# An own list scheduler, smaller first token groups, batched folds and reshaped v reads in a fused attention and GLU block

## The chip, the cores and the metric

The kernel runs on one core of one Trainium2 chip. The metric is the device time of one execution in microseconds (us), inputs and outputs in device memory. Most executions of a kernel agree within about one per cent (the widest fast runs here are 270.24 to 273.89 us). Now and then one execution takes about 1.4 ms; such a run counts as slow and stays out of all comparisons.

PE is the matmul engine (TensorE), PEld its weight loads, DVE the VectorE, ACT the ScalarE, POOL the GpSimd; SPq is the sequencer of the sync engine, which issues the DMAs of this kernel in order.

## The reference, cut to what matters

Sizes: 2048 tokens, model width 512, 32 heads of 16, FFN width 1792, all bfloat16. `_layernorm` has no weights.

```python
mod = (silu(c) @ w_mod).reshape(1, 6, 1, -1)       # sa, ca, ga, sb, cb, gb: one row of 512 each
h = _layernorm(x) * (1 + ca) + sa
x = x + ga * A(h, wqkv, wo)          # attention: every token sees itself and the tokens
                                     # 2, 4, ..., 14 before it (8 keys), softmax over these
h = _layernorm(x) * (1 + cb) + sb
x = x + gb * B(h, w_gate, w_up, w_down)            # (gelu(h @ w_gate) * (h @ w_up)) @ w_down
```

## The kernel before: the parts that the argument touches

Tokens are worked in four groups of 512. q, k and v stand transposed (features on partitions). A key shifted by 2 tokens is a column offset, so the logits of one attention are products of q with shifted k on VectorE, and then sums over the features of a head, made by PE with a 0/1 matrix of 32 columns. Four such narrow matmuls stand side by side in the array. I call four of them a *fold*.

```python
for j in range(4):                                   # attention, logits
    for wg in range(2):
        pq = prodpool.tile([P, 4, SG], BF16, name="pq", tag="prod")
        nc.vector.tensor_tensor(out=pq[:], in0=<q, broadcast>, in1=<k at 4 shifts>, op=ALU.mult)
        for r in range(4):                           # one fold
            nc.tensor.matmul(LT[wg][32 * r:32 * r + 32, :], lhsT=M[:], rhs=pq[:, r, :],
                             start=(j == 0), stop=(j == 3), tile_position=(0, 32 * r))
```

For the weighted sum of v, the heads have to stand on other partitions and v at four shifts. So v goes to DRAM and is read back, four transfers of 128 partitions for a group:

```python
nc.sync.dma_start(out=scr[:], in_=vT[:])
for j in range(4):
    src = bass.AP(scr.tensor, scr.offset + 2 + j * row, [[2, 4], [16 * row, H], [4 * row, 4], [1, VW]])
    nc.sync.dma_start(out=vRj[:], in_=src)           # 4 shifts x 32 heads x 4 features x 520 tokens
```

The scale `gb` is multiplied into the down projection once, on VectorE, within the first group's FFN:

```python
if sg == 0:
    nc.vector.tensor_tensor(out=WdP[:, ft, :], in0=WdP[:, ft, :], in1=gbB[:], op=ALU.mult)
```

The sequence of the groups, which the language's own scheduler then refines:

```python
for sg in range(NSG):
    emit_attention(sg)
    if sg == 0:
        emit_qkv(1); emit_ln1(2); emit_qkv(2); emit_ln1(3)
    elif sg == 1:
        emit_qkv(3)
    if sg >= 1:
        emit_ffn(sg - 1)
emit_ffn(NSG - 1, last=True)
```

## Time and profile before

| | before |
|---|---|
| median of the fast runs | 303.7 us |
| span of the profiled run | 302.1 us |
| PE busy | 264.5 us |
| first matmul of the FFN | 83.1 us |
| end of the last matmul | 298.4 us |

These lines are from the page of the kernel before: PE's busy time and instruction count, then busy tenths in 40 slices of 7.6 us, and the granted PE clock in tenths.

```profile
PE 264.5 (88%) x1476; PEld 113.3 (38%) x1476; DVE 172.9 (57%) x305; ACT 142.0 (47%) x238; POOL 18.1 (6%) x41
PE   7696986128399999998999899899989989999995
PEclk9699899555669999999999999999999999999999
```

From slice 12 on (counted from 1) PE is nearly full. The hole is in slices 7 to 11, and the clock is low in slices 8 to 12: what PE does there it does at 5 or 6 tenths of full speed. The windows view puts numbers to it. Its columns are busy us and instructions of PE, weight loads, DVE, ACT and POOL, then granted clock, DMA share and GB/s.

```profile
40.00:50.00 10.00, 8.64 (x54) 4.03 (x53) 5.06 (x6) 6.98 (x12) 0.23 (x1) 1.00 0.27 89
50.00:60.00 10.00, 2.03 (x16) 0.44 (x15) 4.76 (x4) 1.39 (x3) 1.04 (x1) 0.68 0.51 141
60.00:70.00 10.00, 3.08 (x13) 0.75 (x14) 4.63 (x4) 0.78 (x2) 0.00 (x0) 0.50 1.05 331
70.00:80.00 10.00, 6.72 (x29) 1.89 (x27) 8.26 (x16) 0.00 (x0) 0.70 (x1) 0.67 0.22 70
```

Neither PE nor DVE is full between 50 and 70 us, so both wait. The chain of work that ended last (start, duration, what) names the reason:

```profile
25.36 9.28 DMA scr<-vT
...
37.72 6.75 SPq L258
44.51 20.31 DMA vR<-scr
64.94 1.24 DVE pv L318
```

v of the first group is ready at 25.4 us, and its last piece is back at 64.8. Meanwhile the DMA moves only 89 GB/s (40 to 50 us).

Last, how a fold sits among other matmuls in PE's timeline (start, duration, operation, count):

```profile
159.18 1.04 PE L346 MATMUL g_ps<-h2T,Wg 128*128 128x512 bf16 x4
160.18 0.40 PE L276 MATMUL LT_1543<-pq,Mph 128*32 128x512 bf16 x4
160.51 1.04 PE L350 MATMUL u_ps<-h2T,Wu 128*128 128x512 bf16 x4
```

Read such lines by their starts, for matmuls overlap. Four gate matmuls after one another advance 0.866 us elsewhere in this timeline; here the fold starts 1.00 us after them, and the next group 0.33 us after the fold. A fold in a row of folds advances 0.2165 us. A lone one costs 0.33 + 0.13 = 0.46.

### The profile page before, as it was taken

The page shows a single profiled execution, that of the slowest core. Times are in us where ns is not written, and L with a number is a line of the kernel's source. Part 1 is how long each engine was busy: PE and PEld are TensorE (multiplying, and loading weights), DVE is VectorE, ACT ScalarE, POOL GpSimd, SP SyncE. Part 2 cuts the span into 40 slices and gives each one's busy share as a digit, 9 for nine tenths or more (in the row PEclk, how much of TensorE's full clock was granted, in tenths as well). Part 3 has the DMA queues.
Part 4 walks back from the last instruction along what each step waited for, and adds up shares of the span by engine and source line. Part 5 has one row for each costly group of instructions (what it writes and reads, how often), then busy time and mean ns, then how long its engine had stood idle before and what let it go on. Part 6 is the DMA issues. An engine that isn't in the chain of part 4 may idle for free.

```text
span 302.1 us, 3849 instructions
## 1 busy us (share of the span) xinstructions
PE 264.5 (88%) x1476; PEld 113.3 (38%) x1476; DVE 172.9 (57%) x305; ACT 142.0 (47%) x238; POOL 18.1 (6%) x41
## 2 busy tenths in 40 slices
PE   7696986128399999998999899899989989999995
PEld 3353342002144544344443333344333444444442
DVE  4481747347998328996228599843859852122221
ACT  1366364100168797646305864440685462166700
POOL 6120001000111000002000000200000010000000
PEclk9699899555669999999999999999999999999999
DMA  7999422694222122231220012100000000100000
GB/s 209 383 284 277 150 85 92 165 318 169 59 90 86 67 82 86 96 143 45 76 64 35 0 30 78 36 20 35 17 2 1 0 2 17 53 0 3 0 35 35
DMA packets 21032, 25.87 MB, mean 86 GB/s; under 512 B 661, under 2 KB 19350, under 8 KB 21014
## 3 DMA queue, kind: packets, MB, share of 16 engines
q1 hardware_dynamic: 21012, 25.63, 27.4%
q8 instruction: 11, 0.18, 0.3%
q14 instruction: 7, 0.06, 0.1%
q10 hardware_dynamic: 2, 0.00, 0.0%
HBM read 21.37 MB, written 4.26 MB: 85 GB/s over the span
## 4 chain that ended last, share of the span: by engine, by line
PE 65%; DMA 12%; DVE 11%; SPq 4%; ACT 3%; POOL 2%; issue 1%; POOLq 0%; DVEq 0%; ACTq 0%
PE u_ps L350 13%; PE y_ps L368 12%; PE qkv_ps L246 10%; PE g_ps L346 9%; DMA vR<-scr 7%; PE y_psb L368 4%; PE g_psq L346 4%; PE x_ps L329 4%; SPq L258 3%; PE o_ps L321 3%; DMA scr<-vT 3%; DVE st L183 3%; PE hTp L200 3%; DVE x_sg L331 2%; DMA wm<-in_w_mod_dram 2%; POOL rstd L187 2%
## 5 line engine op out<-in xcount | busy, mean ns | idle before, releaser
L350 PE MATMUL u_ps<-h2T,Wu 128*128 128x512 bf16 x224 | 62.6, 383 | 0.0
L246 PE MATMUL qkv_ps<-hT,wqkv 128*128 128x512 bf16 x192 | 49.3, 397 | 1.7 <-DVE hT L204 1.3
L346 PE MATMUL g_ps<-h2T,Wg 128*128 128x512 bf16 x168 | 49.3, 387 | 0.9 <-ACT h2T L207 0.9
L353 ACT ACTIVATE gl<-g_ps 128x512 bf16<-128x512 f32 x42 | 25.4, 604 | 42.6 <-PE g_ps L346 40.0
L318 DVE TENSOR_TENSOR pv<-e,vR 128x2048 bf16<-128x2048 bf16 x32 | 37.0, 1219 | 11.7 <-DMA vR<-scr 11.6
L273 DVE TENSOR_TENSOR pq<-qT,kT 128x2048 bf16<-128x2048 bf16 x32 | 37.9, 1212 | 6.4 <-PE LT_471 L276 6.4
L355 ACT CAST ub<-u_ps 128x512 bf16<-128x512 f32 x56 | 33.1, 591 | 18.0 <-PE u_ps L350 18.0
L357 DVE TENSOR_TENSOR hht<-gl,ub 128x512 bf16<-128x512 bf16 x56 | 23.0, 419 | 30.7 <-ACT ub L355 30.2
L368 PE MATMUL y_ps<-WdP,hht 128*128 128x512 bf16 x168 | 36.9, 379 | 0.0
L368 PEld LDWEIGHTS <-hht 128*128 128x128 bf16 x224 | 21.9, 98 | 26.2
L346 PEld LDWEIGHTS <-Wg 128*128 128x128 bf16 x224 | 21.0, 99 | 25.8 <-issue 5.3
L350 PEld LDWEIGHTS <-Wu 128*128 128x128 bf16 x224 | 20.7, 98 | 25.5 <-issue 5.1
L246 PEld LDWEIGHTS <-wqkv 128*128 128x128 bf16 x192 | 20.8, 117 | 23.8 <-issue 8.2
L321 PE MATMUL o_ps<-pv,F_157 128*32 128x512 bf16 x128 | 13.7, 416 | 14.5 <-DVE pv L318 14.4
L371 DVE TENSOR_TENSOR ot<-y_ps,x_sg 128x512 bf16<-128x512 f32 x12 | 8.3, 691 | 26.2 <-PE y_ps L368 21.6
L183 DVE BATCH_NORM_STATS2 st<-x_sg 128x6 f32<-128x512 bf16 x32 | 20.9, 672 | 3.8 <-DMA x_sg<-in_A_x_dram 3.8
L187 POOL TENSOR_TENSOR rstd<-rstd,neghalf 128x4 f32<-128x4 f32 x8 | 10.6, 1330 | 187.6 <-DVE rstd L186 187.6
L323 ACT CAST oT<-o_ps 128x512 bf16<-128x512 f32 x16 | 9.4, 586 | 23.2 <-PE o_ps L321 23.2
L329 PE MATMUL x_ps<-woP,oT 128*128 128x512 bf16 x64 | 18.8, 434 | 0.7 <-ACT oT L323 0.7
L207 ACT ACTIVATE h2T<-hTp,modT,scl 128x512 bf16<-128x512 bf16 x16 | 11.6, 787 | 14.7 <-PE hTp L200 14.6
L353 ACT ACTIVATE gl<-g_psq 128x512 bf16<-128x512 f32 x14 | 8.4, 597 | 14.6 <-PE g_psq L346 14.6
L346 PE MATMUL g_psq<-h2T,Wg 128*128 128x512 bf16 x56 | 14.4, 379 | 0.0
(134 smaller groups left out, 214.1 us busy)
## 6 DMA issues: line engine op xcount, KB each, us to landing
vR<-scr SPq DMA_DIRECT2D x16, 520.0 KB
wm<-in_w_mod_dram SPq DMA_DIRECT2D x6, 512.0 KB
scr<-vT SPq DMA_DIRECT2D x4, 528.0 KB
out_dram<-ot SPq DMA_DIRECT2D x16, 128.0 KB
Wg<-in_B_w_gate_dram SPq DMA_DIRECT2D x1, 1792.0 KB
Wu<-in_B_w_up_dram SPq DMA_DIRECT2D x1, 1792.0 KB
WdP<-in_B_w_down_dram SPq DMA_DIRECT2D x1, 1792.0 KB
wqkv<-in_A_wqkv_dram SPq DMA_DIRECT2D x3, 512.0 KB
```

Of the source, the lines that this page charges most:

```text
L183: nc.vector.bn_stats(out=st[:, c4, :], in_=xt[:, c4, :])
L246: nc.tensor.matmul(ps[:], lhsT=wqkv[:, dt, blk * D + j:(blk + 1) * D:4], rhs=hT[:, dt, :], start=(dt == 0), stop=(dt == DT - 1))
L273: nc.vector.tensor_tensor(out=pq[:], in0=_ap(qT[:, j, :], [[0, 4], [1, SG]]), in1=_ap(kT[:, j, :], [[2, 4], [1, SG]], offset=HALO - 6 - 8 ...
L318: nc.vector.tensor_tensor(out=pv[:], in0=_ap(e[:, wg, :], [[0, 4], [1, SG]]), in1=vR[j][:, :, 8 - 8 * wg:8 - 8 * wg + SG], op=ALU.mult)
L321: nc.tensor.matmul(o_ps[32 * d4:32 * d4 + 32, :], lhsT=F1[:], rhs=pv[:, d4, :], start=(wg == 0), stop=(wg == 1), tile_position=(0, 32 * d4))
L329: nc.tensor.matmul(x1_ps[:], lhsT=oT[:, j, c4 * P:(c4 + 1) * P], rhs=woP[:, j, :], start=(j == 0), stop=(j == 3))
L346: nc.tensor.matmul(g_ps[:], lhsT=Wg[:, dt, ft * P:(ft + 1) * P], rhs=h2T[:, dt, :], start=(dt == 0), stop=(dt == DT - 1))
L350: nc.tensor.matmul(u_ps[:], lhsT=Wu[:, dt, ft * P:(ft + 1) * P], rhs=h2T[:, dt, :], start=(dt == 0), stop=(dt == DT - 1))
L353: nc.scalar.activation(out=gl[:], in_=g_ps[:], func=ACT.Gelu_apprx_tanh)
L355: nc.scalar.copy(out=ub[:], in_=u_ps[:])
L357: nc.vector.tensor_tensor(out=hht[:], in0=gl[:], in1=ub[:], op=ALU.mult)
L368: nc.tensor.matmul(y_ps[:], lhsT=hh[ft][:, c4 * P:(c4 + 1) * P], rhs=WdP[:, ft, :], start=(ft == 0), stop=(ft == FT - 1))
```

## The change

The intent: plan every engine's order beforehand with an own list scheduler, bring the first FFN work forward with two half-size groups, cut PE's switches between folds and full matmuls, and read v back faster. Nearly every line of the kernel is rewritten, so only the core of the diff stands here; `[...]` marks cuts.

```diff
+class Plan:                     # every operation is recorded with engine, assumed us, reads, writes, priority
+    def order(self):            # list scheduling: of all ready operations the one that can start first
+        [...]
+            us = o.us
+            if o.table is not None and o.table != table:
+                table, us = o.table, us + 1.3                 # ACT changes its function table
+            engines[o.eng] = at + us
+            if o.dma:
+                pipe = max(pipe, at + us) + o.dma             # one DMA pipe, 385 GB/s if not said otherwise
+                o.end = pipe + 2.0
+    def emit(self):
+        placed = self.order()
+        with self.tc.manual_schedule():                       # this order and no other
+            for o in placed: [...] o.fn()
-    NSG = S // SG
+    GROUPS = [(0, 256), (256, 256), (512, 512), (1024, 512), (1536, 512)]

-        for j in range(4):
-            src = bass.AP(scr.tensor, scr.offset + 2 + j * row, [[2, 4], [16 * row, H], [4 * row, 4], [1, VW]])
-            nc.sync.dma_start(out=vRj[:], in_=src)
+            for r in range(4):                                # one transfer per shift, 32 partitions each
+                lastv = dma(P * njv * (n + 8) * 2, lambda scr=scr, r=r, t=t: nc.sync.dma_start(
+                    out=t[32 * r:32 * r + 32, :, :, :].rearrange("p a b c -> p (a b) c"),
+                    in_=bass.AP(scr.t.tensor, scr.t.offset + 2 + 2 * r, [[4 * njv * row, H], [row, 4 * njv],
+                                                                         [1, n + 8]])), [...] bw=200e3)

+            pe(1.05, fold, r=pq + [M], w=LT, pri=p)           # 16 matmuls of 512 or 32 of 256: four folds

-            if sg == 0:
-                nc.vector.tensor_tensor(out=WdP[:, ft, :], in0=WdP[:, ft, :], in1=gbB[:], op=ALU.mult)
+                gp(1.0, lambda ft=ft: nc.gpsimd.tensor_tensor(out=WdP[:, ft, :], in0=WdP[:, ft, :], in1=gbB[:],
+                                                              op=ALU.mult), [...] pri=500)

+    def late_loads(after):      # big weights behind the first group's v reads
+        [...Wg, Wu, w_mod block 5, tokens 1024-1535, tokens 1536-2047, WdP...]
+        for b in range(nb):     # the exponentials of a group, one operation for each half
+            act(0.5, lambda b=b: nc.scalar.activation([...] func=ACT.Exp), [...] pri=p, table="exp")
```

Groups of 256 run their matmuls at 256 columns, two per PSUM bank, so the evictions keep their size.

## The prediction

> **What bounds it now.** TensorE, after a starved beginning. The page gives PE 264.5 us busy of 302.1. Back to back, a 512-column matmul advances 0.2165 us in the timeline. The groups list 928 of them (gate/up 448, down 224, qkv 192, output projection 64): 201 us. Folds at that pitch, four side by side, are 64 x 0.2165 = 14 us; transposes, broadcasts, sums and modulation about 15. So PE needs about 230 us at full clock.
>
> In the windows view 50-60 and 60-70 us hold only 2.0 and 3.1 us of PE work, and the granted clock is 0.50 to 0.68 from 50 to 80. The first gate matmul starts at 83.1; from the first qkv matmul at 12.0 until then PE did about 33 us of full-clock work: 38 us lost. The chain of waits says why: writing v takes 25.4 to 34.7, the reads back are held in the sync queue to 44.5, the last lands at 64.8. From 90 us on PE is about 97% busy, 6 us of gaps.
>
> **What the change does.**
> 1. v read back. The old pattern's slowest dimension is 4. The Trainium skill, "DMA: Bandwidth & Descriptors" (why a DMA increments its semaphore by 16), says the number of DMA engines is the largest up to 16 that divides both sides' slowest dimension: 4 here, 16 for the new 32-partition reads. The trace agrees: DMA share 0.27, 89 GB/s at 40-50 us, against 1.10 and 352 GB/s at 10-20. I expect under 8 us from write-issue to last landing for 256 tokens, instead of 39.
> 2. Half-size first groups: 8 products of 1.21 us before the first normalised output instead of 16; first gate matmul at 45 to 52 us instead of 83. Qkv of groups 1 and 2 partly fills PE; VectorE limits this stretch (two attentions with norms, about 17 us each).
> 3. Folds in fours. A lone fold between gate matmuls takes 0.33 us and delays its neighbour 0.13: 0.45 against 0.22. Sixteen batches instead of some 45 lone folds: 9 us of PE, on the critical path after 83 us.
> 4. Fixed order: perhaps 2 us of gaps less; but where its modelled durations are wrong, an in-order engine stalls.
> 5. Added: 256-column matmuls (weight loads of 98 ns against about 108, nearly hidden), another exp/gelu table pair (1.28 us each; ScalarE has room). WdP scaling moves to GpSimd: 14 products. "SBUF — State Buffer" says a GpSimd operation and a two-input VectorE one lock each other out; no trace line here shows it. I estimate +2 us.
>
> **Sum.** First qkv at 11 + PE work 230 + batch switches 3 + opening losses 16 + later gaps 4 + tail 3.5 = 267.5. From the other side: 303.7 - 22 (opening loss 38 to 16) - 9 - 1.5 (earlier start) - 2 + 2 = 271. I predict **268 us, 257 to 281**; faster by over 2%: 0.94, within 2%: 0.04, slower: 0.02.
>
> **What would show each step.** Right: first gate matmul at 45-52 us, VectorE waiting for v under 4 us (11.6 now), no 10 us window after 45 us below 7 us of PE, batches of 16 folds in about 1.0 us, PE busy 245-252 us. Wrong: VectorE waiting for v because its read sits behind the big weight loads; PE waiting on WdP from GpSimd; single PE gaps over 1.5 us in mid-run; 256-column matmuls pitched well over 0.11 us.
>
> **What would make it wrong.** Faster: opening loss below 8 us (PE filled by qkv and norms). Slower: GpSimd/VectorE lockout lengthening the opening, or the second group's v late behind 7 MB of weights.

## The result, and the profile after

The result is correct. Its median is 277.95 us (277.48 to 278.48) against 303.66 for the three fast runs of the kernel before (303.45 to 304.77; the fourth took 1423 us). The ratio is 0.9145, 95% interval 0.9109 to 0.9181. A ratio is the mean time of one kernel's fast runs over that of the other's of the same rounds, so it is not quite the ratio of the medians that are quoted.

From the page of the changed kernel:

```profile
PE 248.6 (90%) x1693; PEld 132.3 (48%) x1716; DVE 179.3 (65%) x304; ACT 152.5 (55%) x252; POOL 43.5 (16%) x65
PE   8497897488696999999998999999889999999994
PEclk9779999959998899999999999999999999999999
```

The hole is smaller but not gone. The same windows, and one more:

```profile
40.00:50.00 10.00, 8.59 (x76) 4.25 (x79) 7.49 (x10) 4.77 (x9) 0.24 (x1) 1.00 1.07 367
50.00:60.00 10.00, 4.88 (x57) 2.75 (x50) 9.90 (x24) 5.37 (x9) 7.13 (x9) 0.71 0.89 246
60.00:70.00 10.00, 9.23 (x92) 7.96 (x91) 9.92 (x20) 7.15 (x12) 7.72 (x7) 0.94 1.16 203
70.00:80.00 10.00, 7.81 (x64) 4.17 (x65) 10.00 (x9) 4.28 (x9) 8.40 (x6) 1.00 0.36 65
80.00:90.00 10.00, 7.77 (x48) 3.53 (x45) 9.97 (x16) 5.60 (x10) 2.21 (x2) 0.92 0.64 136
```

DVE (third pair) is full from 50 to 90 us while PE is not: the opening is now bound by DVE. DVE never waits for v any more (11.6 us in the kernel before). The first FFN matmul starts at 57.2 us instead of 83.1. A batch of folds in PE's timeline:

```profile
118.49 1.05 PE L620 MATMUL o_ps<-pv,F_160 128*32 128x512 bf16 x16
119.47 1.05 PE L657 MATMUL u_ps<-h2T,Wu 128*128 128x256 bf16 x8
```

By the starts, four folds take 0.98 us, 0.245 each. The matmuls in front advance 0.97 us instead of 0.87, so with this delay, which the 0.46 of a lone fold includes too, it is 0.27 each.

Three things in this trace were not planned, and each became an experiment.

**GpSimd beside VectorE.** These are DVE's lines, and then GpSimd's at the same time; the last column of a DVE line is its count:

```profile
66.92 1.22 DVE L610 TENSOR_TENSOR pv<-e,vR 128x2048 bf16<-128x2048 bf16 x1
68.06 1.38 DVE L669 TENSOR_TENSOR hht<-gl,ub 128x512 bf16<-128x512 bf16 x1
69.36 2.18 DVE L610 TENSOR_TENSOR pv<-e,vR 128x2048 bf16<-128x2048 bf16 x1
71.46 1.37 DVE L669 TENSOR_TENSOR hht<-gl,ub 128x512 bf16<-128x512 bf16 x1
```

```profile
67.19 11.21 POOL L705 TENSOR_TENSOR WdP<-WdP,gbB 128x512 bf16<-128x512 bf16 x7
```

The same `hht` product takes 0.42 us a little earlier (at 66.58) and the same `pv` product 1.22. With GpSimd's products running beside them, each is 0.95 us longer.

**The function table.** ACT's timeline at the third attention:

```profile
142.02 1.28 ACT L566 ACT_TABLE_LOAD   x1
143.32 0.60 ACT L566 ACTIVATE e<-LT 128x512 bf16<-128x512 f32 x1
...
147.12 0.62 ACT L666 ACTIVATE gl<-g_ps 128x512 bf16<-128x512 f32 x1
147.75 1.28 ACT L566 ACT_TABLE_LOAD   x1
149.05 0.60 ACT L566 ACTIVATE e<-LT 128x512 bf16<-128x512 f32 x1
```

The two exponentials of one attention are 5.7 us apart, with gelus between, so the table is changed four times instead of twice. PE waits for ACT here: 0.88 us in front of an up projection at 152.08.

**Loads that come late for a fixed order.** The chain of the changed kernel:

```profile
32.70 14.87 DMA x_sg<-in_A_x_dram
...
47.60 1.28 DVE st L413 x2
```

DVE's next instruction (`st`) is the first step of the normalisation of tokens 1024 to 1535, whose load sits behind two big weights; DVE waits 2.51 us for it. PE waits too: 1.36 us for the last modulation block, up to 46.13, and only behind that in its order comes the first group's output projection at 47.00. The residual add of that group follows at 48.80, behind two `st` in DVE's order.

### The profile page after: what moved, and what is told of

Same layout as the page of the kernel before. It is cut to its first block, busy times and chain, and to the rows that moved or that the text cites. A ratio compares the mean times of both kernels' runs of the same rounds, so it can differ in the third digit from the quotient of the medians.

```text
span 276.6 us, 4380 instructions
## 1 busy us (share of the span) xinstructions
PE 248.6 (90%) x1693; PEld 132.3 (48%) x1716; DVE 179.3 (65%) x304; ACT 152.5 (55%) x252; POOL 43.5 (16%) x65
## 4 chain that ended last, share of the span: by engine, by line
PE 65%; DVE 11%; DMA 10%; ACT 5%; issue 4%; SPq 4%; DVEq 0%; ACTq 0%
PE y_ps L679 17%; PE u_ps L657 15%; PE g_ps L657 14%; PE qkv_ps L473 6%; DMA x_sg<-in_A_x_dram 5%; DMA wm<-in_w_mod_dram 5%; PE x_ps L634 4%; DVE xn L422 3%; PE LT L530 2%; DVE st L413 2%; PE tp L432 2%; PE o_ps L620 2%; DVE pq L514 2%; SPq L314 1%; ACT gl L666 1%
## 5 line engine op out<-in xcount | busy, mean ns | idle before, releaser
L657 PE MATMUL u_ps<-h2T,Wu 128*128 128x512 bf16 (+1 forms) x277 | 58.2, 341 | 3.0 <-ACT gl L666 2.7
L657 PE MATMUL g_ps<-h2T,Wg 128*128 128x512 bf16 (+1 forms) x275 | 58.7, 344 | 0.6 <-ACT ub L668 0.5
L679 PE MATMUL y_ps<-WdP,hht 128*128 128x512 bf16 x217 | 50.6, 380 | 0.4
L473 PE MATMUL qkv_ps<-hT,wqkv 128*128 128x512 bf16 (+1 forms) x236 | 45.8, 348 | 3.8 <-DMA wqkv<-in_A_wqkv_dram 2.7
L419 POOL TENSOR_TENSOR rstd<-rstd,neghalf 128x2 f32<-128x2 f32 x16 | 14.9, 942 | 157.7 <-DVE mv L415 83.9
L438 ACT ACTIVATE h2T<-tp,modT,scl 128x512 bf16<-128x512 bf16 (+1 forms) x20 | 12.8, 690 | 30.9 <-PE tp L432 30.9
L514 DVE TENSOR_TENSOR pq<-qT,kT 128x2048 bf16<-128x2048 bf16 x24 | 28.4, 1220 | 0.0
L604 DVE TENSOR_TENSOR pv<-e,vR 128x2048 bf16<-128x2048 bf16 x24 | 28.3, 1220 | 0.0
L413 DVE BATCH_NORM_STATS2 st<-x_sg 128x6 f32<-128x512 bf16 x32 | 20.8, 681 | 10.8 <-DMA x_sg<-in_A_x_dram 10.7
L705 POOL TENSOR_TENSOR WdP<-WdP,gbB 128x512 bf16<-128x512 bf16 x14 | 19.3, 1406 | 1.1 <-DMA WdP<-in_B_w_down_dram 1.1
L422 DVE TENSOR_SCALAR xn<-x_sg,mv,rstd 128x512 bf16<-128x512 bf16 x32 | 15.7, 532 | 2.7 <-POOL rstd L419 2.5
L432 PE MATMUL tp<-ident,xn 128*128 128x128 bf16 x128 | 10.6, 221 | 5.3 <-DVE xn L422 4.8
```

What stands on the lines that cost most here:

```text
L413: dve(0.62, lambda i=i, st=st, c0=c0: nc.vector.bn_stats(out=st[:, i, :], in_=x[g, c0 + i]), r=[x.key(g, c0 + i)], w=[(st, i)], pri=p)
L422: dve(0.36, lambda i=i, xn=xn, mv=mv, rstd=rstd, c0=c0: nc.vector.tensor_scalar(out=xn[:, i, :], in0=x[g, c0 + i], scalar1=mv[:, i, 0:1], ...
L473: nc.tensor.matmul(ps[:, j - j0, :], lhsT=wqkv[:, dt, b * D + j:(b + 1) * D:4], rhs=hT[g][:, dt, 0:n], start=(dt == 0), stop=(dt == DT - 1))
L514: dve(1.16, lambda j=j, wg=wg, t=pq[m]: nc.vector.tensor_tensor(out=t[:], in0=_ap(q[g][:, j, 0:n], [[0, 4], [1, n]]), in1=_ap(k[g][:, j, : ...
L604: dve(1.16, lambda jj=jj, jl=jl, wg=wg, t=pv[m]: nc.vector.tensor_tensor(out=t[:], in0=_ap(e[:, wg, :], [[0, 4], [1, n]]), in1=vR[g][jj][: ...
L657: nc.tensor.matmul(ps[:, ft - f0, :], lhsT=Wt[:, dt, ft * P:(ft + 1) * P], rhs=h2[g][:, dt, 0:n], start=(dt == 0), stop=(dt == DT - 1))
```

## The experiments

Twelve kernels ran, all with three timed rounds against the kernel before. Medians are those of the fast runs. The kernel before had medians of 303.57, 303.86 and 304.59 us. The change itself had been timed separately, beside its own runs of the kernel before (303.66), so compare by the ratios where a per cent matters. All twelve passed the comparison with the reference. `a_memset` computes a wrong down projection and passed too: with these inputs the FFN adds next to nothing to x (in the reference, setting `w_down` to zero changes no output by more than 5e-7, where the mean size is 0.04). So passing says little about the FFN of any of these kernels.

| label | what | median us | ratio to before |
|---|---|---|---|
| (the change) | | 277.95 | 0.9145 |
| b_v16 | before, v read on 16 DMA engines | 291.82 | 0.9625 |
| a_v4 | change, v read the old way | 288.34 | 0.9500 |
| a_512 | change, four groups of 512 | 290.21 | 0.9560 |
| a_single | change, folds one by one | 284.48 | 0.9373 |
| a_tile | change, order not fixed | 278.06 | 0.9157 |
| a_dve | change, WdP products on DVE | 269.77 | 0.8887 |
| a_memset | change, WdP products made memsets | 270.65 | 0.8903 |
| a_exp_pin | change, exponentials side by side | 274.48 | 0.9039 |
| a_loads_pin | change, two loads earlier | 276.14 | 0.9104 |
| a_mend | a_dve + a_exp_pin + a_loads_pin | 266.78 | 0.8791 |
| a_replan | the three, planned anew, 300 GB/s | 268.24 | 0.8838 |
| a_replan2 | the same, 250 GB/s | 270.59 | 0.8928 |

### b_v16: the v read alone

```diff
-            src = bass.AP(scr.tensor, scr.offset + 2 + j * row, [[2, 4], [16 * row, H], [4 * row, 4], [1, VW]])
-            nc.sync.dma_start(out=vRj[:], in_=src)
+            for r in range(4):
+                src = bass.AP(scr.tensor, scr.offset + 2 + 2 * r + j * row, [[16 * row, H], [4 * row, 4], [1, VW]])
+                nc.sync.dma_start(out=vRj[32 * r:32 * r + 32, :, :], in_=src)
```

> The kernel before with only its v reads changed: one 32-partition transfer per shift (16 DMA engines) instead of one 128-partition transfer with slowest dimension 4. Theory (the v read gates the opening): the last v of group 0 lands near 46 us instead of 64.8, the first gate matmul comes near 66-70 instead of 83.1, and the time falls by 11 to 18 us, to 286-293. Rival (the attention's chain on VectorE gates it anyway, and only half-size groups help): under 5 us gained, above 298.

The time fell to 291.82 us, by 11.7. The eight weighted products of the first attention, spread from 46.2 to 67.3 us before, now run without a pause:

```profile
46.22 9.21 DVE L319 TENSOR_TENSOR pv<-e,vR 128x2048 bf16<-128x2048 bf16 x8
```

The first gate matmul came at 70.4 us (83.1 before). So the read was a gate of the opening. The language's scheduler also reordered this kernel somewhat, so a part of the 11.7 may not be the read's.

### a_v4: the v read put back

```diff
-            for r in range(4):
-                [... t[32 * r:32 * r + 32] <- [[4 * njv * row, H], [row, 4 * njv], [1, n + 8]] ...]
+            for jl in range(njv):
+                [... t[:, :, jl, :] <- [[2, 4], [4 * njv * row, H], [njv * row, 4], [1, n + 8]] ...]
```

> The changed kernel with the v reads put back to a slowest dimension of 4; the order of PE, VectorE and ScalarE is the same. Theory (the 16-engine read matters in the changed kernel too): v of the first 256 tokens lands 5 to 10 us later, time 282-288. Rival (half-size groups make v small enough, and VectorE is busy elsewhere): 276-280.

288.34 us, 10.4 more than the change, with PE's order unchanged. DVE's own wait for v is only 3.2 us. The larger part goes another way, which the chain of this run shows:

```profile
39.70 15.26 DMA wm<-in_w_mod_dram
...
55.00 1.89 PE mb_ps L396 x4
56.89 2.76 PE x_ps L634 x8
```

The loads stand behind the v reads in the queue, so the last modulation block lands at 55 us. PE has its row product (`mb_ps`) in front of the first attention's output projection (`x_ps`), and in a fixed order it waits: 7.8 us here, 1.4 in the change. The first gate matmul comes at 67.0 us instead of 57.2.

### a_512: no half-size groups

```diff
-    GROUPS = [(0, 256), (256, 256), (512, 512), (1024, 512), (1536, 512)]
+    GROUPS = [(0, 512), (512, 512), (1024, 512), (1536, 512)]
-    PRI_LN1 = (-960, -30, 3.5, 60, 150)
-    PRI_QKV = (-60, 30, 50, 130, 1050)
+    PRI_LN1 = (-960, 3.5, 60, 150)
+    PRI_QKV = (-60, 50, 130, 1050)
```

> The changed kernel with four groups of 512 and the priorities of the dropped group taken out. Theory (half-size first groups bring the first FFN work forward): first gate matmul at 70-78 us instead of 57, time 286-293. Rival (16-engine v reads and the fixed order bring nearly all): below 281.

290.21 us, 12.3 more than the change, first gate matmul at 77.9. The plan is a different one here (its priorities were tuned for five groups), so the 12.3 hold that too.

### a_single: folds one by one

```diff
-            pe(1.05, fold, r=pq + [M], w=LT, pri=p)
+            for m in range(njv):
+                for wg in range(2):
+                    src_t = pq[2 * m + wg] if n == SG else pq[m]
+                    pe(0.33 * n / 512, lambda m=m, wg=wg, fold=fold: fold(m, wg), r=[src_t, M],
+                       w=[LT[wg * (nb - 1)]], pri=p)
```
The folds of `o_ps` were split in the same way.

> The changed kernel with every fold its own operation for the list scheduler, so that lone folds sit between other matmuls again. Theory (a lone fold costs 0.45 us of PE against 0.22-0.27 in a batch, on the critical path after the opening): PE busy up by 5 to 9 us, time 283-288. Rival (switches are hidden in waits): 276-280.

284.48 us, 6.5 more. PE's busy time rose by 11.8 us to 260.4, more than the time. Part of the switching falls into waits.

### a_tile: the planned sequence, but not fixed

```diff
-        with self.tc.manual_schedule():
+        if True:
```

> The changed kernel's operations handed over in the same planned sequence, but with the language's own scheduler free to reorder them (the fixed order undone, all else kept). Theory (the fixed order itself carries a good part: unbroken fold batches, and the priorities of the opening): time 282-290, PE busy higher by 3 us or more. Rival (the order is worth little beside groups, folds and v reads): 275-280.

278.06 us: the same as the change, within the interval. The theory fell. From 114 us on the fold batches stayed whole (16 matmuls in 1.05 us in PE's timeline, as in the change). In the opening they did not: one batch of 32 matmuls runs as four of 8, at 78.36, 79.67, 80.78 and 82.08 us, and the first gate matmul comes at 59.7 instead of 57.2. DVE's instructions were reordered in many places, and its busy time is 172.7 us instead of 179.3: the new order happens to avoid a part of the collisions described above. So pinning the sequence brings no net gain here; what it is worth without the collisions stays open. What the *planned sequence* is worth against the kernel before's simple loop was not measured by itself; batches and groups cannot be had without some sequence.

### a_dve, a_exp_pin, a_loads_pin, a_mend: the three unplanned costs

`a_dve` puts the products back on VectorE:

```diff
-                gp(1.0, lambda ft=ft: nc.gpsimd.tensor_tensor(out=WdP[:, ft, :], in0=WdP[:, ft, :], in1=gbB[:],
+                dve(0.42, lambda ft=ft: nc.vector.tensor_tensor(out=WdP[:, ft, :], in0=WdP[:, ft, :], in1=gbB[:],
```

> The changed kernel with the 14 WdP products on VectorE again (PE order all but the same). Theory (GpSimd and VectorE lock each other out from 50 to 80 us; VectorE instructions there are about 11 us longer than elsewhere, and the products cost it only 14 x 0.42 = 6 us): VectorE's mean for the normalisation falls from 532 to about 410 ns, the opening shortens, time 271-275.5. Rival (VectorE's length in the opening isn't what limits, or the two costs cancel): 277-279.

`a_exp_pin` and `a_loads_pin` take the planned order and move single operations in it. `o` is placed directly behind `ahead`:

```diff
         placed = self.order()
+        for o, ahead in self.PIN:
+            placed.remove(o)
+            placed.insert(placed.index(ahead) + 1, o)
```

In `a_exp_pin` the second exponential of each attention goes behind the first.

> The changed kernel's order kept, but each attention's second exponential moved directly behind its first, so no gelu stands between. Theory (the planned order pays two extra pairs of table loads, on PE's path near 144-152 and 193-202 us): table loads fall from 12 to 8, time 274-276.5. Rival (ScalarE's slack hides them): 277.3-278.5.

In `a_loads_pin` the last modulation block and then tokens 1024-1535 go behind the first group's v reads, ahead of the big weights.

> The changed kernel's order kept on all compute engines; only the sync queue differs: the last modulation block and tokens 1024-1535 are loaded before the big weights instead of behind 3.7 MB of them. Theory (the in-order VectorE and PE stand waiting for them at 45-48 us, so the first group's output comes late): VectorE's wait for x falls from 10.7 to about 8 us, first gate matmul 2 to 4 us earlier, time 274-276.5. Rival (other waits take their place): 277-279.

`a_mend` does all three.

> All three together: WdP on VectorE, exponentials side by side, the two early loads. If the three are independent the gains add up: 267-272. If they share one wait: no better than the best of the three.

Measured: 269.77, 274.48, 276.14 and 266.78 us. Against the change that is -8.2, -3.5, -1.8 and -11.2. The three singles add up to 13.5, or, by the ratios, 12.3 against 10.8 together; each is uncertain by about 1 us, so an overlap is likely but not shown. `a_dve` gained more than expected (271 to 275.5). In `a_dve`, PE is full from 60 us on:

```profile
60.00:70.00 10.00, 10.00 (x100) 8.38 (x97) 8.27 (x20) 8.39 (x14) 1.34 (x2) 1.00 1.18 200
70.00:80.00 10.00, 10.00 (x74) 5.33 (x74) 9.96 (x18) 5.69 (x11) 1.27 (x1) 1.00 0.54 111
80.00:90.00 10.00, 10.00 (x100) 6.45 (x99) 9.86 (x21) 8.17 (x15) 7.75 (x3) 1.00 0.64 135
```

In `a_exp_pin` the exp and gelu table loads fell from 12 to 8. The edit also brings each second exponential forward; what that alone is worth was not separated from the loads. In `a_loads_pin` the first gate matmul came at 52.8 us, 4.4 earlier, but the time fell by only 1.8, and the 95% intervals of the two ratios overlap (0.9069 to 0.9140 against 0.9109 to 0.9181), so this gain is not clear of the noise. DVE's wait for x hardly changed (10.2 us; 8 was expected), and DVE is still full from 60 to 90 us; most of the earlier start seems to be lost there.

### a_memset: is it GpSimd being busy, or both engines reading?

`a_dve` takes load off GpSimd as well as the collisions, so a rival remained: a busy GpSimd holds up the short GpSimd steps behind it (1/sqrt of the norm, and halo copies, which put the last 16 tokens of a group in front of the next one's k and v). Here GpSimd stays busy but reads nothing.

```diff
-                gp(1.0, lambda ft=ft: nc.gpsimd.tensor_tensor(out=WdP[:, ft, :], in0=WdP[:, ft, :], in1=gbB[:],
-                                                              op=ALU.mult), r=[(WdP, ft), gbB], [...]
+                gp(1.0, lambda ft=ft: (nc.gpsimd.memset(WdP[:, ft, :], 0.002),
+                                       nc.gpsimd.memset(WdP[:, ft, :], 0.001)), r=[(WdP, ft), gbB], [...]
```

> Wrong result on purpose: the 14 WdP products on GpSimd become pairs of GpSimd memsets into the same places (about 1.05 us a pair, no reading), all orders kept. Theory (VectorE and GpSimd block each other when both read): VectorE's normalisation falls from 532 to 400-440 ns, its busy time from 179 to about 168-171 us, time 266-271. Rival (a busy GpSimd holds up the rstd and halo copies that queue behind, whatever it does): 275-279 with VectorE's lengths back to normal.

270.65 us. In the traces, PE, DVE and ACT run the same instructions in the same order as in the change. The groups view by form (operation, shapes, count | busy us, mean ns | idle before and releaser) of the change:

```profile
L669 DVE TENSOR_TENSOR hht<-gl,ub 128x512 bf16<-128x512 bf16 x56 | 26.6, 474 | 40.3 <-ACT ub L668 40.3
L705 POOL TENSOR_TENSOR WdP<-WdP,gbB 128x512 bf16<-128x512 bf16 x14 | 19.3, 1406 | 1.1 <-DMA WdP<-in_B_w_down_dram 1.1
L422 DVE TENSOR_SCALAR xn<-x_sg,mv,rstd 128x512 bf16<-128x512 bf16 x32 | 15.7, 532 | 2.7 <-POOL rstd L419 2.5
L610 DVE TENSOR_TENSOR pv<-e,vR 128x2048 bf16<-128x2048 bf16 x8 | 11.4, 1458 | 0.1
```

of `a_memset`:

```profile
L669 DVE TENSOR_TENSOR hht<-gl,ub 128x512 bf16<-128x512 bf16 x56 | 23.6, 422 | 39.0 <-ACT ub L668 38.9
L705 POOL MEMSET WdP<- 128x512 bf16 x28 | 14.9, 554 | 1.0 <-DMA WdP<-in_B_w_down_dram 0.2
L422 DVE TENSOR_SCALAR xn<-x_sg,mv,rstd 128x512 bf16<-128x512 bf16 x32 | 14.5, 494 | 2.5 <-POOL rstd L419 2.4
L610 DVE TENSOR_TENSOR pv<-e,vR 128x2048 bf16<-128x2048 bf16 x8 | 9.5, 1220 | 0.5 <-DMA vR<-scr 0.5
```

and of `a_dve`:

```profile
L669 DVE TENSOR_TENSOR hht<-gl,ub 128x512 bf16<-128x512 bf16 x56 | 23.6, 421 | 36.8 <-ACT ub L668 36.7
L422 DVE TENSOR_SCALAR xn<-x_sg,mv,rstd 128x512 bf16<-128x512 bf16 x32 | 11.6, 404 | 4.0 <-POOL rstd L419 3.9
L610 DVE TENSOR_TENSOR pv<-e,vR 128x2048 bf16<-128x2048 bf16 x8 | 9.5, 1219 | 1.7 <-DMA vR<-scr 1.7
```

With memsets, the two-input products (`hht`, `pv`) are back at their free length, though GpSimd is still busy. The normalisation (`xn`, one tensor input) is not: 494 ns (400 to 440 was expected) against 404 free and 532 with the products. That fits the Trainium skill, "SBUF — State Buffer" (who interferes with whom): a VectorE instruction with two SBUF inputs contends with a GpSimd one that reads SBUF and not with one that only writes; single-input operations in a two-port mode contend with both. Whether `xn` runs in such a mode no view here shows. The rival (275 to 279 us) is out, and the time of `a_memset` (7.3 us below the change) puts the larger part of the 8.2 us on collisions of reads. It is no exact share: in `a_memset` the collisions of `xn` remain, and DVE doesn't have the products to do.

### a_replan, a_replan2: the mends as inputs of the plan

The exponentials of an attention became one operation, the products went to VectorE, the two loads got priorities ahead of the weights, and the plan's assumed DMA rate was set to 300 and to 250 instead of 385 GB/s.

> The three mends as inputs of the plan instead of moved afterwards, and the plan's DMA rate 300 instead of 385 GB/s. Theory (the plan was good except where its model was wrong): at or below the version with the three mends, 262-267. Rival (the hand-tuned priorities fit the old model only): 268-274.

> The same with 250 GB/s, to see how much the plan's result hangs on that number: within 1.5 us of the 300 GB/s plan if it hardly matters, over 3 us away if it is a lottery.

268.24 and 270.59 us (ratios 0.8838 and 0.8928): both better than the change, neither better than moving three things by hand in the old plan (266.78). The first theory (262 to 267) failed; `a_replan2` is clearly slower than `a_mend`, while the interval of `a_replan` (0.8785 to 0.8891) overlaps that of `a_mend` (0.8774 to 0.8807). The two plans differ by 2.4 us in the medians for a number that no kernel instruction holds, which is between the two forecasts, and their intervals overlap as well, so the question of the lottery stays open. The priorities seem to fit the old model; that is a reading, not a test. One of the four runs of `a_replan` was the 1.4 ms kind, and the profile was taken of that one, so nothing is read from its profile here about the fast state.

## Why the prediction was right or wrong

The measured 277.95 us lie inside the range 257 to 281, but 10 us above the 268 predicted. By the opposite test, undoing one part at a time, the main mechanisms stand.

- **v reads on 16 engines: right in kind.** Undone: +10.4 us; alone on the old kernel: -11.7. DVE's wait for v went from 11.6 us to none. The step "under 8 us from write-issue to last landing" was wrong: the write is issued at 20.90 us and lands at 26.74, the four reads are issued from 26.76 on, and the third of them lands at 34.33 (the trace lacks the fourth's landing). The products that use them start at 35.9 without a wait. So it took between 13 and 15 us: 5.8 for the write, 4.8 to 6.2 for each read.
- **Half-size groups: right in kind.** Undone: +12.3 us. The first gate matmul at "45 to 52 us" was too early; it is 57.2 (56.7 in `a_dve`, without the collisions), and "no 10 us window below 7 us of PE" failed at 50-60 us (4.88).
- **Folds in fours: right.** 0.98 us a batch; PE busy 248.6 us, inside 245 to 252. "9 us" was too much: undone, it costs 6.5.
- **Fixed order, "perhaps 2 us": no net gain** (`a_tile`). What was feared of it did happen: stalls where the model was wrong.
- **256-column matmuls: right.** Eight advance 0.87 us, 0.109 each.
- **The step that failed is the term for GpSimd: "I estimate +2 us".** The 2 us stood for the whole of step 5; the products on GpSimd alone measured 8.2 (`a_dve`). The mechanism was named, and named again as the first danger on the slow side, but it was sized far too small; the prediction doesn't say how the 2 us were worked out. What counts is the effect on an engine that has no slack: DVE's busy time is 179.3 us with the 14 products elsewhere and 173.0 with them on DVE (5.1 us), which makes 11.4 us of waiting inside DVE's instructions. Counted instruction by instruction in the trace, against the median of the same form, it is 9.3, all of it between 50 and 80 us, where DVE bounds the opening. The prediction was also wrong that no trace line showed it: in the profile before, the same small GpSimd copy (`vT`) takes 0.24 us twice and 1.04 once, at 50.53, beside a two-input product of DVE that runs from 50.25 to 51.48.
- **"Another exp/gelu table pair; ScalarE has room": wrong by the kind of cost.** There were 12 loads where 8 suffice, and undoing the four gained 3.5 us (`a_exp_pin`). ACT is only 55% busy; latency counted, not its busy share.
- **Late loads** were not in the sum (they were named as a danger for v): 1.8 us, not clear of the noise (`a_loads_pin`).

Put together: 268, plus 6.2 (8.2 instead of 2), plus 3.5, plus 1.8, is 279.5, less 2.3 because the three together gave less than their sum (11.2 against 13.5): 277.2. With the three undone the kernel takes 266.8, close to the sum that was predicted. That both come out so near is in part luck: the folds (9 predicted, 6.5 undone) and the fixed order (2, none) were overrated by 4.5 us together, which this reckoning leaves out and for which no run here shows what made up for it. The opening loss of "16 us" is where all but the table loads sit: setting the predicted other terms against the span of 276.6 us leaves about 25 for it (an estimate).

The whole gain can't be split without remainder: the three parts undone one at a time sum to 29.2 us, the change gained 25.7. They overlap, and two of those kernels were planned anew.

## What to carry to other kernels

Before work is moved to an idle engine, ask whether it shares a memory port with the engine that bounds the stage; an estimate of the moved work's own length misses the cost, which is what the bounding engine loses. A planned in-order sequence is only as good as its weakest assumed duration: compare the plan with a trace, look for the instructions in front of a stalled one that could have waited, and mend those by hand. When a transfer is slow, look at the slowest dimension of both access patterns before looking at its bytes.

## What the Trainium skill lacked or had wrong

- "DMA: Bandwidth & Descriptors" (why a DMA increments its semaphore by 16) was right on how a pattern's slowest dimension sets the number of engines, as far as time shows it: 4 instead of 16 cost 10.4 us here (`a_v4`). It gives no price for the loads that queue behind: here the modulation block landed at 55 us, and PE's wait for it grew from 1.4 to 7.8 us.
- "SBUF — State Buffer" (two separate sides) says that the loser waits for the whole instruction of the other. It does not say that the loser can wait for several. In `a_dve` a GpSimd copy of 64 elements per partition took 7.32 us (0.24 elsewhere) while DVE ran 16 two-input products back to back (POOL spans are rough; a weaker case is in the change, where a `kT` copy of the same size took 2.56 us at 20.03 beside DVE's products from 19.01 to 22.50):

```profile
82.37 7.32 POOL L460 COPY vT<-vT 128x64 bf16<-128x64 bf16 x1 [2.11 <-ACT vT L478]
```

- "ScalarE: Activation LUTs" (what ACT_TABLE_LOAD costs) gives 1283 ns for the load, as measured here, and a drain of about 1380 ns more for each switch. No drain shows here: the gelu at 147.12 ends by 147.74, the load starts at 147.75 and the exponential at 149.05, 1.30 us later.
- "TensorEngine Tiling (Array Packing)" (key properties) says that a change of tiling mode drains the array, without a number. Here a lone fold costs 0.46 us instead of 0.2165, about 0.25 us for the two changes; four folds in one batch cost 1.08 (with the delay in front) instead of 0.87.
- No page explains the rare slow runs. One run of `a_replan` and one of the kernel before took 1421 and 1423 us. In the profile of the former, matmuls are slow throughout while the records show a granted clock of 1.0: 37 down-projection matmuls take 48.90 us, 1.32 each against 0.2165. The other engines are as fast as ever there (`pq` on DVE 1220 ns, `gl` on ACT 597). "TensorE: Matmul & The Clock Gate" (seeing it yourself) does warn that the clock records can't be fully trusted. The cause stays open. The line is from the chain of that run:

```profile
1341.84 48.90 PE y_ps L681 x37
```
